# A fused attention and softplus layer: pairing the first blocks of two sequences, with their bias on TensorE and a new order of the work

## The chip, the cores and the metric

The kernel runs on one core of one Trainium2 chip. The metric is device time in microseconds (us) from start to end of one execution, lower is better; three executions of the kernel before gave a median of 213.77 us. The engines are TensorE (PE; its weight loads are shown apart as PEld), VectorE (DVE), ScalarE (ACT), GpSimd (POOL), and SyncE (SP), which here does nothing but issue DMAs. The DMAs that move the data run on 16 DMA engines.

## What is computed

Attention over 4 sequences of 768 tokens with 8 heads of 64, where a token sees the last 96 tokens of its sequence and the first 8 (the global ones), with a linear distance bias per head; then two matrix products with a softplus between them.

```
scores = q @ k^T / sqrt(64)
rel = pos[:, None] - pos[None, :]
is_global = pos[None, :] < 8
is_local = (rel >= 0) & (rel < 96)
dist = where(is_global & ~is_local, 96, abs(rel))
scores = where(is_global | is_local, scores - slope[h] * dist, -1e9)
a = softmax(scores) @ v                 # (4, 8, 768, 64)
x = a.transpose(0, 2, 1, 3).reshape(3072, 512)
h = x @ w_in                            # w_in (512, 2048)
g = max(h, 0) + log1p(exp(-abs(h)))     # softplus
out = g @ w_out                         # w_out (2048, 512)
```

All inputs and the output are float32; the matrix products run in bf16.

## The kernel before

**Tiling.** The 3072 tokens are cut into 24 blocks of 128, six to a sequence. Two blocks are a unit, loaded and transposed together; `UNITS` lists the 12 units in the order in which they are worked. Block n is the n-th in that order, and units and groups have the same numbers: group g of the second half of the layer takes blocks 2g and 2g+1. A block attends to itself and to the block before it in its sequence (256 keys); the first block of a sequence has only itself (128 keys). The 8 global tokens are copied, by `globals_k` (gk) and `globals_v` (gv), into places of the block before that are out of the local window.

**Order.** Nothing is scheduled when the program is built. `ORDER` is one list of words "operation:engine" (P, V, A, G, S for PE, DVE, ACT, POOL, SP), and each engine gets its operations in just this order; an operation that must wait holds up all that stand behind it on its engine. `PLACED` makes the list a table, and dependencies follow from the keys that each operation reads and writes. The names, with unit or block and part as numbers:

- `ldq`, `ldk`, `ldv`: loads of a unit; `win`, `wout`: loads of one of 8 pieces of 512 KB of w_in or w_out (two of them make a column chunk of w_in); `cin`, `cout`: their casts to bf16 (L627).
- `castq`, `castk`, `castv`: casts to bf16. `trq`, `trk`: transposes of q and k, on PE for units 0 to 2 (L740, evicted from PSUM by `cpq`, `cpk`, L747), by DMA later (L763, L770).
- `sb`: the bias put into PSUM by a matmul with the identity (L812, L856); `sc`: scores (L822, L875); `z`: the bias added by DVE where it is not in PSUM (L901); `ex`: the exponential on ACT (L835, L908); `pv`: times v (L927); `nm`: the division (L938, L939); `xt`, `xc`: x transposed into `XT`.
- `a g.p`: one of 8 parts of h = x w_in for group g (L985), `e` and `ln` on ACT: softplus as log(1 + exp(h)) (L1000, L1011); `b`: g w_out (L1032 for groups 0 and 1, L519 later, where seven products of sums take the place of eight, with `ws` and `ka`, L414 and L449, making the sums).
- `fill`: 35 matmuls of zeros (L1145), put where PE was thought to be idle.
- `biasFalse`, `biasTrue`: tiles of bias per head, for first blocks and for others, built on DVE, ACT and POOL.

**Loads.** A unit's q, k or v is 512 KB. For units 0 to 2 (`WIDE`) q and k come in two loads of 256 KB, each partition getting 8 tokens of one head, 2 KB in one run (L582). All else is one load with 512 B runs (L592). In the first stretch the queue holds, in this order, with the two halves of q0 on ACT's queue and the rest on SP's:

```
k0.1 k0.0 q1.0 v0 q1.1 k1.0 win0 k1.1 win1 v1 k2.0 win3 win2 k2.1 q2.0 q2.1
win5 win4 win7 win6 wout0 wout1 v2 wout3 wout2 wout4 wout5 q3 wout6 k3 wout7
```

Later loads are held back by `gates`: each waits for a named product of an earlier group. Loaded data lie in 13 slots (`raw`), used in turn.

**The first stretch on PE**, cut after b0.0.2:

```
fill0 ... fill9 trk0 trq0 fill10 sb0 fill11 ... fill14 sc0 fill15 sb1.0 fill16 sc1.0 sb1.1 pv0.0 sc1.1 fill17 pv0.1
fill18 trq1 fill19 trk1 fill20 pv1.0 pv1.1 fill21 fill22 xt0 sc2 fill23 fill24 fill25 xt1 fill26 fill27 sc3.1 sc3.0
fill28 a0.1 pv2.0 a0.0 fill29 a0.3 fill30 pv2.1 trq2 trk2 xt2 fill31 a0.2 fill32 fill33 pv3.0 a0.5 a0.4 pv3.1 sc4
a0.7 xt3 a0.6 b0.0.0 a1.1 a1.0 b0.0.2
```

a0.0 and a0.1 need both win0 and win1 cast, a0.2 and a0.3 win2 and win3, and so on: a0.7 is the first that needs win6. b0.0.0 needs wout0.

Of the kernel before, what the change touches and what calls it, by code (L numbers as in the profile page):

```python
# [68 lines left out]
ldq0.1:A iota:G ldk0.1:S ldq0.0:A ldk0.0:S dl1a:V blank:V table:A ldq1.0:S dl1c:V fill0:P dl0a:V ldv0:S dl0b:V  # L69
fill1:P dl0c:V ldq1.1:S fill2:P dl1e:V d0:G ident:G fill3:P ldk1.0:S biasTrue2:A d0e:V fill4:P ones:G fill5:P  # L70
biasFalse2:V fill6:P biasFalse7:A biasFalse5:G biasFalse1:V castk0.1:A fill7:P biasFalse6:V biasTrue0:A fill8:P
biasFalse3:A win0:S castk0.0:V biasTrue4:A fill9:P castq0.1:A castq0.0:V ldk1.1:S trk0.0:P biasTrue7:V castq1.0:A
win1:S biasFalse0:V biasFalse4:A trq0.0:P ldv1:S cpk0.0:V fill10:P ldk2.0:S sb0.0:P cpq0.0:A biasTrue3:V fill11:P
castv0.00:G win3:S cpk0.1:V cpq0.1:A fill12:P fill13:P biasTrue1:A fill14:P biasTrue6:G biasTrue5:V sc0.0:P fill15:P
sb1.0:P castv0.11:G ex0.0:A win2:S castv0.01:V fill16:P ex0.1:A sc1.0:P castv0.10:G ldk2.1:S castq1.1:V sb1.1:P
ex1.0:A pv0.0:P sc1.1:P nm0.0:V fill17:P ldq2.0:S ex1.1:A castk1.0:V pv0.1:P fill18:P castk1.1:V ldq2.1:S trq1.0:P
nm0.1:V fill19:P trk1.0:P cpq1.1:V fill20:P cin1:G win5:S pv1.0:P cpk1.0:A cpq1.0:V pv1.1:P fill21:P cpk1.1:A
fill22:P nm1.0:V xt0:P nm1.1:V sc2.0:P fill23:P castv1.11:A castv1.01:G win4:S fill24:P z2.1:V fill25:P xt1:P
gv4.0:A castv1.10:G fill26:P win7:S z2.0:V fill27:P sc3.1:P xc1:A xc0:V cin0:G sc3.0:P ex2.0:A fill28:P z3.0:V
ex2.1:A win6:S castv1.00:G a0.1:P cin3:A castk2.0:G z3.1:V wout0:S pv2.0:P a0.0:P cin2:G e0.1:A wout1:S fill29:P  # L80
nm2.0:V a0.3:P e0.0:A castq2.0:G ldv2:S castk2.1:V ln0.0:A castq2.1:G wout3:S fill30:P pv2.1:P nm2.1:V gk4:G ex3.0:A
trq2.0:P trk2.0:P cin5:G wout2:S cpq2.1:V xt2:P e0.3:A fill31:P a0.2:P cpk2.0:V xc2:A gv4.1:G wout4:S cin4:V
fill32:P fill33:P e0.2:A pv3.0:P cpk2.1:V a0.5:P ex3.1:A cin7:G wout5:S nm3.0:V a0.4:P cpq2.0:V e0.5:A ln0.1:A
pv3.1:P cin6:V sc4.0:P gv8.1:G nm3.1:V a0.7:P ldq3:S e0.4:A z4.0:V ln0.2:A cout0:G wout6:S xt3:P a0.6:P xc3:V e0.7:A
gk8:G z4.1:V b0.0.0:P e0.6:A cout1:G ldk3:S a1.1:P ln0.3:A ws0.1:V a1.0:P ws0.6:V e1.1:A b0.0.2:P castv2.01:G
wout7:S ws0.4:V e1.0:A a1.3:P ex4.1:A castv2.00:G ws0.3:V a1.2:P ldv3:S e1.3:A gk5:G fill34:P ex4.0:A castv2.10:G
sc5.0:P ws1.4:V a1.5:P cout3:G e1.2:A z5.0:V cout2:A pv4.0:P a1.4:P cout4:G e1.5:A nm4.0:V sc5.1:P ln1.0:A ws2.6:V
pv4.1:P b0.0.4:P ws0.7:V a1.7:P e1.4:A gv5.0:V ln1.1:A ws2.7:G z5.1:V b1.0.0:P b1.0.2:P cout5:A b0.0.6:P ws1.7:V
castv2.11:G b1.0.4:P castq3.0:A a1.6:P gv5.1:V cout6:G ldq4:S nm4.1:V b1.0.6:P ex5.0:A trq3:S b0.1.0:P ws2.4:V xt4:P
e1.6:A b0.0.8:P ws1.1:V castk3.0:A b0.0.10:P b0.1.2:P ws3.6:V b0.1.4:P xc4:A trk3.0:S cout7:V b0.1.6:P e1.7:A  # L90
b0.0.12:P ws2.1:V ln1.2:A b0.0.14:P ws1.3:V pv5.0:P b0.1.8:P ex5.1:A nm5.0:V b0.1.10:P ldk4:S b1.0.8:P ws2.3:V
ln1.3:A gk6:G b0.1.12:P ws1.6:V castv3.11:G ldq5:S pv5.1:P b0.1.14:P trk3.1:S oc0.0.0:V castq4.0:A b1.0.10:P ws3.3:G
nm5.1:V b1.0.12:P oc0.1.0:A b1.0.14:P trq4:S xt5:P oc1.0.0:V sc6.0:P castv3.01:G xc5:A gv6.1:A b1.1.0:P castv3.00:G
ldk5:S z6.0:V a2.1:P gv6.0:A castk4.0:G a2.0:P z6.1:V ex6.0:A trk4.0:S pv6.0:P ex6.1:A b1.1.2:P nm6.0:V b1.1.4:P
e2.0:A st1.0.0:S gk7:G pv6.1:P castv3.10:G e2.1:A ldv4:S sc7.0:P nm6.1:V ldv5:S ln2.0:A ws3.4:G a2.2:P trk4.1:S
z7.0:V b1.1.6:P e2.2:A gv7.0:G a2.3:P z7.1:V xt6:S ex7.0:A gv7.1:G b1.1.8:P castq5.0:G e2.3:A pv7.0:P sc8.0:P
ex7.1:A nm7.0:V gv8.0:G a2.5:P z8.0:V ln2.1:A castk5.0:G pv7.1:P b1.1.10:P e2.5:A nm7.1:V a2.4:P castv4.00:G ex8.0:A
z8.1:V xt7:S castv4.01:G a2.7:P e2.4:A castv4.11:V b1.1.12:P ex8.1:A ldq6:S ws3.1:V pv8.0:P a2.6:P st0.1.0:S ln2.2:A
nm8.0:V trq5:S gk9:G b1.1.14:P castv4.10:V e2.6:A pv8.1:P sc9.0:P e2.7:A nm8.1:V gv9.1:G trk5.0:S castv5.00:A a3.0:P
oc1.1.0:V castv5.11:G ln2.3:A ws3.7:G z9.0:V a3.1:P st1.1.0:S xt8:S e3.0:A b2.3:P ka2.7:V ex9.0:A a3.2:P gv9.0:V  # L100
st0.0.0:S ka2.5:G z9.1:V e3.1:A ldv6:S b2.4:P ldk6:S e3.2:A ka2.1:V trk5.1:S ex9.1:A pv9.0:P a3.3:P castv5.10:G
gk10:A a3.4:P ln3.0:A nm9.0:V ka2.6:V pv9.1:P e3.3:A sc10.0:P nm9.1:V gv10.0:G oe2.a:A a3.5:P e3.4:A z10.1:V ka2.2:G
xt9:S b2.1:P e3.5:A ex10.1:A a3.6:P ldq7:S oe2.1:V ldv7:S gv10.1:G a3.7:P ln3.1:A z10.0:V gk11:G castv6.11:G b2.5:P
# [45 lines left out]
WIDE = (0, 1, 2)  # L149
# [1151 lines left out]
```

## Time and profile before

| What | Value |
|---|---|
| Runs | 213.77, 213.84, 212.75 us; median 213.77 |
| The profiled execution | 212.39 us, of which the span from first to last instruction is 210.6 us |
| TensorE clock granted over the span | 0.999 |
| Start to 10 us: PE busy, DMA share | 7.03 us, 0.81 |
| 10 to 20 us | 9.39 us, 1.06 |
| 20 to 30 us | 8.98 us, 1.07 |
| 30 to 40 us | 10.00 us, 1.10 |
| 70 to 80 us | 8.70 us, 1.12 |
| 80 to 200 us | 9.89 us or more in every 10 |
| First part of h = x w_in (a0.1) | starts at 18.69 us |
| a0.7 | starts at 28.94 us |
| Last filler | starts at 35.28 us |
| Load of 256 KB of q or k, issue to landing, median | 7.5 and 6.6 us |
| Load of 512 KB of w_in, issue to landing, median | 9.3 us |

The busy time of PE includes the fillers, and neighbouring matmuls overlap in it, so a full stretch is one in which nothing more fits in, not one without waste. The DMA share is the mean over the 16 DMA engines of the time in which their packets were under way; with several at once it can be over 1. In a timeline, each row is a start, a duration, an engine, a line of the kernel and an operation, "out<-in", and in brackets how long the engine sat idle ahead of it and what ended that.

### The profile page before, as it was taken

The page shows a single profiled execution, that of the slowest core. Times are in us where ns is not written, and L with a number is a line of the kernel's source. Part 1 is how long each engine was busy: PE and PEld are TensorE (multiplying, and loading weights), DVE is VectorE, ACT ScalarE, POOL GpSimd, SP SyncE. Part 2 cuts the span into 40 slices and gives each one's busy share as a digit, 9 for nine tenths or more (in the row PEclk, how much of TensorE's full clock was granted, in tenths as well). Part 3 has the DMA queues.
Part 4 walks back from the last instruction along what each step waited for, and adds up shares of the span by engine and source line. Part 5 has one row for each costly group of instructions (what it writes and reads, how often), then busy time and mean ns, then how long its engine had stood idle before and what let it go on. Part 6 is the DMA issues. An engine that isn't in the chain of part 4 may idle for free.

```text
span 210.6 us, 5494 instructions
## 1 busy us (share of the span) xinstructions
PE 201.3 (96%) x2211; PEld 164.4 (78%) x2211; DVE 156.1 (74%) x287; ACT 174.6 (83%) x248; POOL 105.5 (50%) x113
## 2 busy tenths in 40 slices
PE   5898899999999979999999999999999999999993
PEld 2465687655778868888988988888899889888883
DVE  5779699988788965889888878858883976023494
ACT  5768799998999998978789999896997999775710
POOL 4347668745954763455415783502126849129040
PEclk9999999999999999999999999999999999999999
DMA  5999999999999999999999599955641103400205
GB/s 196 337 355 386 387 357 363 336 209 242 221 304 191 221 214 271 240 166 288 209 170 225 180 181 272 146 124 128 153 99 28 25 5 102 150 0 0 103 0 199
DMA packets 70136, 40.98 MB, mean 195 GB/s; under 512 B 30432, under 2 KB 61664, under 8 KB 70112
## 3 DMA queue, kind: packets, MB, share of 16 engines
q1 hardware_dynamic: 69680, 39.99, 76.2%
q10 hardware_dynamic: 432, 0.66, 0.9%
q8 instruction: 17, 0.28, 0.6%
q14 instruction: 7, 0.06, 0.1%
HBM read 27.26 MB, written 6.29 MB: 159 GB/s over the span
## 4 chain that ended last, share of the span: by engine, by line
PE 68%; DMA 13%; POOL 5%; ACT 5%; DVE 4%; issue 2%; ACTq 0%; SPq 0%; POOLq 0%; DVEq 0%
PE h_ps L985 31%; PE o_ps L519 20%; DMA raw<-in_k_dram 5%; PE s_ps L875 4%; PE x_ps L927 4%; PE s_ps L1032 3%; DMA kT<-kb 3%; DMA raw<-in_q_dram 3%; DMA qT<-qb 2%; PE o_ps L1032 2%; POOL raw L449 2%; ACT pb L908 2%; ACT e L1000 2%; ACT g L1011 1%; POOL g L449 1%
## 5 line engine op out<-in xcount | busy, mean ns | idle before, releaser
L985 PE MATMUL h_ps<-XT,w_in_bf 128*128 128x256 bf16 x768 | 95.5, 273 | 1.5 <-POOL w_in_bf L627 1.3
L985 PEld LDWEIGHTS <-w_in_bf 128*128 128x128 bf16 x768 | 72.4, 98 | 13.1 <-POOL w_in_bf L627 1.9
L1000 ACT ACTIVATE e<-h_ps 128x512 f32<-128x512 f32 x96 | 60.2, 636 | 14.3 <-PE h_ps L985 13.9
L1011 ACT ACTIVATE g<-e 128x1024 bf16<-128x1024 f32 x48 | 50.0, 1057 | 0.4
L901 DVE TENSOR_TENSOR z<-s_ps,biasA 128x1024 f32<-128x1024 f32 x38 | 45.8, 1216 | 3.4 <-PE s_ps L875 2.0
L908 ACT ACTIVATE pb<-z 128x1024 bf16<-128x1024 f32 (+1 forms) x44 | 43.2, 992 | 1.1 <-DVE z L901 1.0
L519 PEld LDWEIGHTS <-g 128*128 128x128 bf16 x320 | 30.8, 98 | 3.6
L449 POOL TENSOR_TENSOR raw<-g 128x1024 bf16<-128x1024 bf16 x11 | 23.5, 2142 | 19.3 <-ACT g L1011 12.8
L677 POOL CAST vb<-raw 64x512 bf16<-64x512 f32 x31 | 20.4, 660 | 11.0 <-DMA raw<-in_v_dram 9.1
L449 POOL TENSOR_TENSOR g<-g 128x1024 bf16<-128x1024 bf16 x9 | 19.5, 2171 | 12.3 <-DVE raw L449 9.7
L793 POOL COPY vb<-vb 4x512 bf16<-4x512 bf16 x16 | 9.8, 612 | 31.7 <-PE x_ps L927 30.6
L519 PEld LDWEIGHTS <-raw 128*128 128x128 bf16 x240 | 23.1, 98 | 2.9
L519 PE MATMUL o_ps<-raw,raw 128*128 128x256 bf16 x192 | 24.1, 273 | 0.0
L519 PE MATMUL o_ps<-raw,g 128*128 128x256 bf16 x160 | 20.1, 273 | 0.0
L927 PEld LDWEIGHTS <-pb 128*128 128x128 bf16 x352 | 16.4, 98 | 4.3 <-ACT pb L908 0.9
L939 DVE TENSOR_TENSOR xs<-x_ps,rcp 128x256 bf16<-128x256 f32 x40 | 17.0, 424 | 1.4
L449 DVE TENSOR_TENSOR raw<-g 128x1024 bf16<-128x1024 bf16 x19 | 15.6, 827 | 2.7 <-ACT g L1011 2.7
L519 PE MATMUL o_ps<-w_out_bf,g 128*128 128x256 bf16 x128 | 16.1, 272 | 0.0
L927 PE MATMUL x_ps<-vb,pb 128*128 128x65 bf16 x304 | 15.8, 193 | 0.0
L938 DVE RECIPROCAL rcp<-x_ps 128x4 f32<-128x4 f32 x40 | 7.1, 179 | 10.3 <-PE x_ps L927 10.1
L1145 PE MATMUL x_ps<-blank 128*128 128x512 bf16 x35 | 12.2, 436 | 2.2 <-DVE blank L1084 2.2
L483 DVE TENSOR_TENSOR osb<-osb,o_ps 128x512 f32<-128x512 f32 x8 | 5.5, 686 | 10.3 <-PE o_ps L519 8.1
(109 smaller groups left out, 227.6 us busy)
## 6 DMA issues: line engine op xcount, KB each, us to landing
raw<-in_v_dram SPq DMA_DIRECT2D x12, 512.0 KB, 6.3
out_dram<-osb SPq DMA_DIRECT2D x22, 256.0 KB, 2.5
raw<-in_q_dram SPq DMA_DIRECT2D x9, 512.0 KB, 5.3
raw<-in_k_dram SPq DMA_DIRECT2D x9, 512.0 KB, 5.1
raw<-in_moe_w_in_dram SPq DMA_DIRECT2D x8, 512.0 KB, 9.3
raw<-in_moe_w_out_dram SPq DMA_DIRECT2D x8, 512.0 KB, 9.4
raw<-in_k_dram SPq DMA_DIRECT2D x6, 256.0 KB, 6.6
raw<-in_q_dram SPq DMA_DIRECT2D x4, 256.0 KB, 7.5
```

The source lines that it names most:

```text
L449: (nc.vector if eng == "DVE" else nc.gpsimd).tensor_tensor(dst, a[0], b[0], ALU.subtract)
L519: nc.tensor.matmul(psum(j), lhs[:, f // 2, f % 2, :], w(f), start=(f == 0 and not (chain and j in "267")), stop=(f == 7), skip_group_check ...
L677: copy_on[eng](dst, src)
L901: nc.vector.tensor_tensor(z, src, bias, ALU.add)
L908: nc.scalar.activation(pb[:, 0:nr, :].rearrange("p (y a) b -> p y (a b)", y=2), src, AF.Exp, scale=1.0 / root_d)
L927: nc.tensor.matmul(xv[:, h, :], pb[:, 4 * (h % 2) + 2 * part + h // 2 if lone else u_all * (2 * (h % 2) + h // 2) + u, :], vb_of(prev if u ...
L939: nc.vector.tensor_tensor(xs[:, 4 * part : 4 * part + 4, :], xv[:, :, 0:D], rcp[:][:, :, None].to_broadcast([P, 4, D]), ALU.mult,)
L985: last = nc.tensor.matmul(hv[:, j, :], w_in_bf[:, m, fb * P : fb * P + P], XT[g % NXG][:, m, :], start=(m == 0), stop=(m == NM - 1),)
L1000: nc.scalar.activation(e[:, p % 2, :, :].rearrange("p j (b t r) -> p (j b) r t", b=2, r=2), hb[:].rearrange("p (a r t) -> p a r t", a=4, r=2),
L1011: nc.scalar.activation(gt[:, 2 * p - 2 : 2 * p + 2, :].rearrange("p a t -> p (a t)"), e[:].rearrange("p a j t -> p (a j t)"), AF.Ln, bias=1.0,
L1032: nc.tensor.matmul(bank(key)[:, 0 : z - a], gt[:, fb, ns * P : ns * P + P], w_out_bf[:, fb, a:z], start=(fb == 0), stop=(fb == NFB - 1),)
L1145: nc.tensor.matmul(x_ps[:], blank[:, 0:P], blank[:])
```

## The change

It pairs the blocks differently. `UNITS` now names the first block itself, and a unit that starts at a block below 2 takes the same block of the next sequence as its second one. Unit 0 is the first block of sequences 0 and 1, unit 1 that of sequences 2 and 3, unit 2 the second block of sequences 0 and 1, unit 7 that of sequences 2 and 3; the others are two neighbours as before. Blocks 0 to 3 are thus the four first blocks (before, blocks 0, 2, 12 and 18 were), and all four get their bias on TensorE, from the first-block tile, with one score operation each; before, block 1 got the wider tile on TensorE, and blocks 2 and 3 were added on DVE.

A q or k half load of units 0 to 2 is as large as before, 256 KB in runs of 2 KB, but is drawn from two sequences: its source pattern runs over 8 pairs of sequence and head, then 16 groups of 8 tokens, where it ran over 32 groups, then 4 heads. Partitions are numbered accordingly, and the eviction of the transposes reads PSUM in another order. The v loads of units 0 to 2, and all three of unit 7, are cut in two, one sequence and 64 partitions each, with keys of their own (`rawx`); `half_users` adds these to what later users of a slot wait for.

```diff
-UNITS = [(0, 0), (1, 0), (0, 1), (0, 2), (1, 1), (1, 2), (2, 0), (2, 1), (2, 2), (3, 0), (3, 1), (3, 2)]
+UNITS = [(0, 0), (2, 0), (0, 1), (0, 2), (1, 2), (0, 4), (1, 4), (2, 1), (2, 2), (3, 2), (2, 4), (3, 4)]
...
-PE_BIAS = (0, 1)
+PE_BIAS = (0, 1, 2, 3)
...
-WHOLE = (0, 2, 4, 6, 7, ...)
+WHOLE = (0, 1, 2, 3, 4, 6, 7, ...)
...
-    units = [[(s, 2 * c), (s, 2 * c + 1)] for s, c in UNITS]
+    units = [[(s, b), (s, b + 1) if b > 1 else (s + 1, b)] for s, b in UNITS]
...
+    def half_users(slot):
+        return [u for x in range(2) for u in users(("rawx", slot, x))]
+
+    def src_keys(which, i, slot, xs=range(2)):
+        if units[i][0][1] < 2 and not (i in WIDE and which != "v"):
+            return [("rawx", slot, x) for x in xs]
+        return raw_keys(slot)
...
         s, b0 = units[i][0]
-        sl = slice(P * b0, P * b0 + W)
+        cross = b0 < 2
+        sl = slice(P * b0, P * b0 + (P if cross else W))
...
                             raw[:, 512 * y : 512 * y + 512],
-                            src[y::2, sl, :].rearrange("h (g r) d -> g h (r d)", r=8),
+                            src[s : s + 2].rearrange("s (h y) t d -> y (s h) t d", y=2)[y, :, sl, :].rearrange(
+                                "x (g r) d -> x g (r d)", r=8
+                            ),
...
+            def ld(dst, rows):
                 return nc.sync.dma_start(
-                    raw[:].rearrange("p (h c) -> p h c", h=H),
-                    src[:, sl, :].rearrange("h (p r) d -> p h (r d)", r=2),
+                    dst.rearrange("p (h c) -> p h c", h=H), rows.rearrange("h (p r) d -> p h (r d)", r=2)
                 )
...
+            if cross:
+                since = half_users(slot) + [u for key in raw_keys(slot) for u in users(key)]
+                for x in range(2):
+                    op(f"ld{which}{i}.{x}", "SP", 0.45, rank + 0.01 * z,
+                       lambda x=x, src=src, raw=raw: ld(raw[64 * x : 64 * x + 64, :], src[s + x, :, sl, :]),
+                       dma=(0.93, 30.0), sync=sync, writes=[("rawx", slot, x)], after=since)
+                continue
...
-        return ("kTa", units[i][0][0] % 2) if first_of(i) else ("kT", later.index(i) % NKT)
+        return ("kTa", units[i][0][0] // 2) if first_of(i) else ("kT", later.index(i) % NKT)
...
-            return NVB + 2 * (units[i][0][0] % 2) + n % 2
+            return NVB + units[i][0][0] + n % 2
...
                     dst[:, :, 64 * r : 64 * r + 64].rearrange("p (x m) (g a) -> p x m g a", x=2, a=4),
-                    tr[:, 512 * r : 512 * r + 512].rearrange("p (a x g m) -> p x m g a", a=4, x=2, g=16),
+                    tr[:, 512 * r : 512 * r + 512].rearrange("p (a x m g) -> p x m g a", a=4, x=2, g=16),
```

`ORDER` is replaced as a whole. The loads of the first stretch are now, with both halves of q0 on ACT's queue as before:

```
v0.0 k0.0 k0.1 k1.0 q1.1 v0.1 q1.0 v1.0 k1.1 v1.1 win0 win1 win3 win2 win4 q2.0
win5 win7 q2.1 k2.0 k2.1 win6 wout2 wout1 v2.0 wout3 wout0 v2.1 wout7 q3 wout5 wout4 k3 wout6
```

and PE's list, cut after b0.0.2:

```
fill0 ... fill3 trq0 fill4 trk0 sb0 fill5 sc0 sb1 sc1 fill6 fill7 fill8 pv0.0 fill9 fill10 trq1 pv1.1 pv0.1 fill11 fill12
trk1 fill13 pv1.0 fill14 fill15 fill16 xt0 fill17 xt1 fill18 ... fill21 a0.0 fill22 sb2 sc2 a0.1 fill23 a0.2 a0.3 pv2.0
fill24 sb3 fill25 sc3 a0.5 pv2.1 a0.4 fill26 xt2 fill27 trq2 fill28 pv3.0 trk2 fill29 fill30 fill31 pv3.1 fill32 a0.7
xt3 a0.6 sc4 a1.1 a1.0 fill33 sc5.0 fill34 a1.3 a1.2 sc5.1 b0.0.0 pv4.0 b0.0.2
```

On POOL cin0 and cin1 now stand together ahead of castv1.11 (before: cin1, then two casts of v1, then cin0); cin6 moves from DVE to POOL, and the eight biasTrue tiles are built behind the exponentials of blocks 0 and 1.

More of the change, by code (lines that the diff above doesn't have):

```diff
@@ L74 @@
[L74 to L88, printed above, removed]
```

164 lines of the change are left out of this document (90 added, 74 removed).

## The prediction

> **What bounds the kernel now.** I read the page first, then the busy time by stretches, the timeline of TensorE and GpSimd over the first 36 us, the waits and the DMA issues.
>
> ```profile
> PE 201.3 (96%) x2211; PEld 164.4 (78%) x2211; DVE 156.1 (74%) x287; ACT 174.6 (83%) x248; POOL 105.5 (50%) x113
> ...
> PEclk9999999999999999999999999999999999999999
> DMA  5999999999999999999999599955641103400205
> GB/s 196 337 355 386 387 357 363 336 209 242 221 304 191 221 214 271 240 166 288 209 170 225 180 181 272 146 124 128 153 99 28 25 5 102 150 0 0 103 0 199
> ```
>
> ```profile
> 18.70:28.90 10.20, 9.18 (x113) 7.54 (x113) 8.09 (x17) 8.56 (x13) 6.46 (x10) 1.00 1.06 382
> 28.90:35.50 6.60, 6.60 (x61) 5.33 (x57) 6.43 (x9) 6.51 (x11) 5.27 (x8) 1.00 1.08 366
> 35.50:77.50 42.00, 41.86 (x453) 30.65 (x452) 36.90 (x62) 40.38 (x56) 27.75 (x33) 1.00 1.15 249
> 77.50:79.10 1.60, 0.30 (x5) 0.07 (x4) 0.13 (x1) 1.57 (x3) 0.52 (x1) 1.00 0.65 145
> 79.10:207.30 128.20, 128.09 (x1440) 112.58 (x1440) 90.35 (x162) 104.86 (x147) 56.92 (x45) 1.00 0.60 138
> ```
>
> ```profile
> 18.69 1.05 PE L985 MATMUL h_ps<-XT,w_in_bf 128*128 128x256 bf16 x8 [0.53 <-POOL w_in_bf L627]
> ...
> 28.94 1.05 PE L985 MATMUL h_ps<-XT,w_in_bf 128*128 128x256 bf16 x8
> ...
> 35.28 0.38 PE L1145 MATMUL x_ps<-blank 128*128 128x512 bf16 x1
> ```
>
> ```profile
> 14.51 1.03 POOL L627 CAST w_in_bf<-raw 128x1024 bf16<-128x1024 f32 x1 [2.72 <-DMA raw<-in_moe_w_in_dram]
> ...
> 23.97 1.04 POOL L627 CAST w_in_bf<-raw 128x1024 bf16<-128x1024 f32 x1 [0.51 <-DMA raw<-in_moe_w_in_dram]
> ...
> 26.76 1.04 POOL L627 CAST w_in_bf<-raw 128x1024 bf16<-128x1024 f32 x1 [1.07 <-DMA raw<-in_moe_w_in_dram]
> ...
> 28.01 0.69 DVE L627 CAST w_in_bf<-raw 128x1024 bf16<-128x1024 f32 x1
> ```
>
> The columns of a stretch are PE, PEld, DVE, ACT and POOL busy, granted clock, DMA share, GB/s. From 28.9 to 207.3 us TensorE is busy all the time but for one wait of 1.3 us at 77.6, at full clock; behind it come only two DVE additions and the last stores (3.3 us). So the end is fixed by two numbers: how late TensorE becomes full, and how much work is then left. Before 35.5 us it does 20 us of real work; the other 15.4 are 35 filler matmuls of 0.216 us each (7.6) and 7.8 of waiting. What it waits for are casts of loaded data, and those wait for the DMA, whose mean share is 0.93 to 1.08 until 35.5 us. **The first 35 us are paced by the arrival of 12 MB, and all that follows by TensorE.**
>
> I turn the GB/s slices (5.265 us each) into a running sum: 1.03 MB at 5.3 us, 2.81 at 10.5, 4.68 at 15.8, 6.71 at 21.1, 8.75 at 26.3. Adding up the loads in queue order gives each its place: v0 ends at 1.84 MB and its first cast starts when the sum is 2.21 (8.79 us); w_in piece 1 ends at 3.67 MB and its cast starts when the sum is 4.22 (14.51 us); piece 5, place 6.82, at 7.84 (23.97); piece 7, place 7.86, at 8.91 (26.76). A load lands once the sum is 0.4 MB, later 0.55 and then 1.0 MB past its place. The last one, piece 6, has place 8.39 and lands by 28.0; its DVE cast (28.01) releases a0.7 at 28.94.
>
> **The change, part by part.**
>
> *Bias on TensorE.* Before: 4 seeds of 256 columns (0.44 us) and 4 of 512 (0.87). After: 16 of 256, 1.75 us. TensorE **+0.44 us**. DVE loses the additions z2 and z3, 1.28 + 2.36 = 3.6 us; at 17.4 to 20.2 us TensorE waits for loads, not for them, so I count nothing, though ex2 and ex3 can start that much sooner.
>
> *Scores, values, transposes, global copies.* Counts are unchanged: four first blocks of 8 score matmuls, twenty others of 16. The eviction reads TensorE's transposed columns in another order, but still 4 values 128 apart at the innermost; nearest rows are DVE 0.68 us, ACT 0.53. Bounds 0 and, at double, 12 x 0.6 us on ACT and DVE inside the load-bound stretch; I take 0.
>
> *v in halves, and unit 7.* Six more SP issues of 0.4 to 0.6 us. Ten issues, not six, precede w_in piece 0 on SP: its issue goes from 4.92 to about 6.9 us. It lay some 7 us in the queue behind other bytes, so this costs nothing while the queue is full, 2 us if it weren't. Behind them on SP only more loads wait. The three extra issues for unit 7 (some 1.5 us of SP near 70 us) come before the transposes for unit 6, whose kind caused the 1.3 us wait at 77.6: 0 to 1.5, taken as 0. Added dependencies only name slots already empty.
>
> *Order of loads.* All twelve q/k halves, v0, v1 and the eight pieces still precede or include piece 6, so its place stays 8.39 MB: equal bytes, 28.0 us. What moves up is little: piece 1 slips to 4.19 MB, landing near 16.1; its POOL cast no longer stands behind castv1, so a0.0 starts near 17.2 instead of a0.1 at 18.69. That lead is gone at a0.7, which again needs piece 6, now cast on POOL (1.04, not 0.69): 29.15 us, **+0.2**.
>
> *Order on TensorE.* What is left once a0.7 starts? Before it, a0.0 to a0.5, six transposes, seeds, scores and xt0 to xt2 are done in both; but before also had sc4.0 (0.55) and all of sc3, pv0 to pv3 with the longer windows: 13.4 us in all, after 12.6, of a total that is 0.44 larger. So 1.3 us more real work follows, and two fillers instead of one (0.22): **+1.5**. wout0 is now the fourth w_out piece, at 10.75 MB: about 35 to 36 us, cast by 37; b0.0.0 comes up near 36.4. At most 0.7 more; I take 0.
>
> *Source pattern of the wide loads.* The twelve q/k half loads of units 0 to 2 keep 256 KB and 2 KB runs, but the outer count of the source goes from 32 (groups of 8 tokens) to 8 (sequence and head), with 16 groups inside. No row of this trace has such a load; all its plain loads and stores have one of 32 or 128, which 16 divides. Lower bound 0: the 256 KB rows as they are (6.6 and 7.5 us to landing). Upper bound: if work is dealt out by the outer count, eight of the 16 engines carry all 3.15 MB, 0.393 MB each instead of 0.197. An engine at 360 to 387 GB/s over 16 moves 0.0225 to 0.0242 MB/us, so the 0.197 MB costs 8.1 to 8.7 us, all ahead of piece 6. A part of it is returned if the laggards, which make the lag grow from 0.4 to 1.0 MB (0.6/0.36 = 1.7 us), are among the idle eight: 6.4. I take this end, since an outer count that 16 divides is the one thing that all the full-rate loads share, at **+7.2**, the middle of 6.4 and 8.1.
> [...]
>
> **Sum.** 7.2 + 0.2 + 1.3 + 0.2 = 8.9 us. Everything behind a0.7 is shifted with it, the later loads too, since those are gated on TensorE's own products. Profiled span 210.6 + 8.9 = 219.5. That execution took 212.39, and the median of the runs is 213.77, 3.17 above the span: **222.7 us**. Own range 219 (a delay of 3.5, if engines that run alone are quicker than any slice here shows) to 225.5 (8.7, and 1.3 more from b0 or unit 7).
>
> **Rivals.**
> *Loads spread as before.* Then only +1.7 remains, and up to 0.7 for wout0: 215.5 to 216.2, with unit 7 worst 217.7. For it: equal bytes and equal runs. Against: the outer count. If the wait at 77.6 also goes, 214.2.
> *Faster.* The 1.0 MB lag is one of uneven engines; v in halves and first blocks first may land piece 6 with the early lag of 0.4 MB, 1.7 us sooner, at 26.3; with its POOL cast a0.7 starts at 27.4, 1.5 sooner. That pays for the 1.5 of work; with the 1.3 saved at 77.6, since other transposes stand there, the span is 209.3, the time 212.5. It decides at a0.7: with that wait gone a start before 28.7 gains, before 27.6 by over 0.5%. For it: in the old order win0 lands near 12 us and its cast waits for castv1 until 17.59. Against: the lag grew while all loads were alike.
> *The change only moves DVE work.* If biases were what held ex2 and ex3, 3.6 us less DVE would show before 20 us; but a0.1 waits on POOL, so no gain: the second case again.
>
> **How the numbers follow.** First case 0.70, second 0.17, third 0.13. About 0.5% (1.07 us) is what a measurement can tell. Slower: 0.70 + 0.8 of the second case = 0.84; the same: the rest of the second and a sixth of the third, 0.05; faster 0.11. The range 214.0 to 225.5 holds most of the first two cases, about 0.8.
>
> **What would show it.** First case: GB/s under 300 in the second and third slices with w_in casts waiting longer on DMA, a0.0 at 20 us or later, a0.7 near 36, or 33 at the quick end, the first score matmul after 10 us (9.44 now), q/k landing times over 9 us early on. Second: a0.0 near 17, a0.7 near 29. Third: a0.7 before 28. From a0.7 on, gaps on TensorE as before; a new wait of over 2 us there (transposes for units 3 to 7, late w_out) would make every sum wrong, as would piece 6 not being what releases a0.7.

## The result, and the profile after

The changed kernel takes **233.91 us** (median of four runs, 232.57 to 235.61) against 213.26 us for the kernel before on the same chip: a ratio of 1.097, with a 95% interval of 1.088 to 1.107. The change makes the kernel slower, as forecast, but by 20.6 us and not by 9; the time lies outside the range of 214.0 to 225.5. Some executions of a kernel come out slower than its others; the ratios and intervals here leave these out, the medians do not.

The profiled execution took 232.57 us with a span of 230.8, against 210.6 before: 20.2 us to be found in the trace. First the page's slices (5.77 us each): TensorE, its granted clock, the DMA share and what the DMA engines moved.

```profile
span 230.8 us, 5493 instructions
...
PE   3095798399999998999999999999999999999993
...
PEclk9999799999999999999999999999999999999998
DMA  4779978999999979899998997996871311300204
GB/s 87 192 190 199 325 242 227 268 277 306 304 174 273 238 207 227 169 222 261 205 182 212 211 249 141 234 247 164 119 113 31 116 26 50 110 25 1 94 19 164
```

In the first four slices 3.9 MB arrive by 23.1 us (5.77 us x 668 GB/s); before, 7.5 MB had. The DMA digits there (4, 7, 7, 9) say that this isn't only engines kept out of work: in the fourth slice they are busy and still move 199 GB/s. From the ninth slice on TensorE is as full as before. The same stretches as in the table of before (PE, PEld, DVE, ACT and POOL busy, granted clock, DMA share, GB/s):

```profile
0.00:10.00 10.00, 1.89 (x4) 0.44 (x4) 2.10 (x8) 2.92 (x6) 3.08 (x12) 1.00 0.55 122
10.00:20.00 10.00, 6.97 (x51) 4.02 (x53) 3.63 (x13) 4.35 (x8) 1.32 (x3) 1.00 0.84 206
20.00:30.00 10.00, 6.63 (x55) 4.36 (x56) 4.26 (x12) 3.72 (x7) 4.33 (x6) 0.83 1.06 282
30.00:40.00 10.00, 9.27 (x95) 6.64 (x95) 4.83 (x14) 8.82 (x15) 2.34 (x3) 1.00 0.78 225
40.00:50.00 10.00, 5.84 (x67) 4.54 (x68) 5.01 (x10) 5.31 (x8) 3.24 (x5) 1.00 1.08 280
```

The timeline of TensorE shows where the time goes: the waits of over 0.4 us in this stretch, behind the one for the first filler, and the starts of a0.0 (29.16) and a0.7 (45.77).

```profile
12.11 1.03 PE L759 MATMUL s_ps<-ident,qb 128*128 128x128 bf16 x8 [6.25 <-DVE qb L664]
...
19.96 0.62 PE L759 MATMUL s_ps<-ident,qb 128*128 128x128 bf16 x8 [0.86 <-DVE qb L664]
...
24.64 1.03 PE L759 MATMUL s_ps<-ident,kb 128*128 128x128 bf16 x8 [3.37 <-POOL kb L664]
...
29.16 1.04 PE L1004 MATMUL h_ps<-XT,w_in_bf 128*128 128x256 bf16 x8
...
43.03 0.62 PE L759 MATMUL s_ps<-ident,kb 128*128 128x128 bf16 x8 [3.09 <-POOL kb L664]
...
45.77 1.05 PE L1004 MATMUL h_ps<-XT,w_in_bf 128*128 128x256 bf16 x8 [1.13 <-POOL w_in_bf L646]
...
53.71 0.59 PE L1051 MATMUL s_ps<-w_out_bf,g 128*128 128x512 bf16 x2 [0.45 <-POOL w_out_bf L646]
```

The three long waits are for casts of q and k, the halves whose source pattern was changed. a0.7 starts at 45.77 instead of 28.94: **16.8 of the 20.2 us are there before a0.7**. The other 3.4 can be read off too. From a0.7 to its end TensorE is busy for 178.5 us instead of 176.9 (1.6), it stands still for 2.97 us instead of 1.55 (1.4), and behind its last matmul pass 3.5 us instead of 3.2 (0.3). The casts that end the three long waits start at 11.63, 23.98 and 42.35 us, each when its load has landed, and the loads are the half loads of q and k. Of all waits of the kernel (total, number, longest) these are the ones for them, first those of the changed kernel, then the largest of the kernel before:

```profile
POOL kb L664 <- DMA raw<-in_k_dram: 13.6, 4, 5.8
...
DVE qb L664 <- DMA raw<-in_q_dram: 11.1, 4, 5.0
```

```profile
POOL qb L645 <- DMA raw<-in_q_dram: 3.1, 1, 3.1
...
DVE kb L645 <- DMA raw<-in_k_dram: 0.7, 2, 0.5
```

### The profile page after: what moved, and what is told of

The parts are those of the page before. It is cut to its first block, busy times and chain, and to the rows that moved or that the text cites. A ratio compares the mean times of both kernels' runs of the same rounds, so it can differ in the third digit from the quotient of the medians.

```text
span 230.8 us, 5493 instructions
## 1 busy us (share of the span) xinstructions
PE 204.9 (89%) x2211; PEld 166.5 (72%) x2219; DVE 159.6 (69%) x283; ACT 173.1 (75%) x244; POOL 111.0 (48%) x117
## 4 chain that ended last, share of the span: by engine, by line
PE 59%; DMA 22%; ACT 7%; DVE 5%; SPq 3%; issue 2%; POOL 1%; DVEq 0%; ACTq 0%; POOLq 0%
PE h_ps L1004 26%; PE o_ps L519 20%; DMA raw<-in_k_dram 6%; DMA raw<-in_moe_w_out_dram 6%; PE x_ps L946 3%; PE s_ps L894 3%; DMA qT<-qb 3%; DMA kT<-kb 3%; DMA raw<-in_q_dram 2%; DMA XT<-xs 2%; ACT e L1019 2%; ACT g L1030 2%; DVE z L920 2%; PE x_ps L519 2%; ACT pb L927 1%
## 5 line engine op out<-in xcount | busy, mean ns | idle before, releaser
L1019 ACT ACTIVATE e<-h_ps 128x512 f32<-128x512 f32 x96 | 59.4, 634 | 19.9 <-PE h_ps L1004 18.9
L920 DVE TENSOR_TENSOR z<-s_ps,biasA 128x1024 f32<-128x1024 f32 x40 | 48.1, 1218 | 4.1 <-PE s_ps L894 4.1
L927 ACT ACTIVATE pb<-z 128x1024 bf16<-128x1024 f32 x40 | 41.7, 1050 | 2.3 <-DVE z L920 2.2
L449 POOL TENSOR_TENSOR g<-g 128x1024 bf16<-128x1024 bf16 x9 | 20.1, 2237 | 23.4 <-DVE raw L449 23.4
L449 POOL TENSOR_TENSOR raw<-g 128x1024 bf16<-128x1024 bf16 x9 | 19.1, 2128 | 23.0 <-ACT g L1030 18.1
L696 POOL CAST vb<-raw 64x512 bf16<-64x512 f32 x31 | 22.1, 714 | 15.5 <-DMA raw<-in_v_dram 11.7
L449 DVE TENSOR_TENSOR raw<-g 128x1024 bf16<-128x1024 bf16 x21 | 17.3, 843 | 1.6 <-ACT g L1030 1.6
L812 POOL COPY vb<-vb 4x512 bf16<-4x512 bf16 x17 | 11.4, 673 | 10.9 <-PE x_ps L946 5.6
L696 ACT CAST vb<-raw 64x512 bf16<-64x512 f32 x8 | 4.9, 617 | 10.8 <-DMA raw<-in_v_dram 9.4
```

The lines of the kernel that those rows point to most:

```text
L449: (nc.vector if eng == "DVE" else nc.gpsimd).tensor_tensor(dst, a[0], b[0], ALU.subtract)
L696: copy_on[eng](dst, src)
L812: copy_on[eng](vb_of(prev)[sl, :, 0:D], vb_of(first)[sl, :, 0:D])
L920: nc.vector.tensor_tensor(z, src, bias, ALU.add)
L927: nc.scalar.activation(pb[:, 0:nr, :].rearrange("p (y a) b -> p y (a b)", y=2), src, AF.Exp, scale=1.0 / root_d)
L1019: nc.scalar.activation(e[:, p % 2, :, :].rearrange("p j (b t r) -> p (j b) r t", b=2, r=2), hb[:].rearrange("p (a r t) -> p a r t", a=4, r=2),
```

## The experiments

The first theory was the prediction's: the new source of the wide loads runs on 8 DMA engines, and the rest costs some 2 us. It leaves 11 us open. The rivals for them were the order of the loads, a wait on SP, the price of the new source on 16 engines, and the halves of v. The expectations name theories by letters; D is that all rows fall in the same halves of 64 KB of memory, F that the halves of v cost the time; G stands for one thing in `b_vhalf` and for another in `b_gap4` and `b_local`. Eighteen kernels were run, each beside the kernel before, which took 211.9 to 212.8 us there. `k16`, `k16_w2`, `k16_b7`, `a_u2`, `b_k4` and `b_vhalf` compute the same as the kernels that they come from; the others read a part of q, k or v from other tokens and serve for their time alone. Their GB/s between 4 and 12 us, the stretch that is most of it wide loads and v, is the quickest way to read them: 342 in the kernel before, 167 in the changed one.

**All 16 engines for the same tokens.** `k16` puts the 16 groups of 8 tokens outermost; the eviction of the transposes restores the order. Same computation.

```diff
-  "x (g r) d -> x g (r d)", r=8
+  "x (g r) d -> g x (r d)", r=8
...
-  tr[...].rearrange("p (a x m g) -> p x m g a", a=4, x=2, g=16)
+  tr[...].rearrange("p (a g x m) -> p x m g a", a=4, x=2, g=16)
```

> The changed kernel with one edit: the source of the twelve q/k half loads runs over 16 groups of tokens outermost and over the 8 pairs of sequence and head inside (partition numbers and the eviction follow). Theory A (the outer count of 8 confines these loads to half the engines, and that is all but about 2 us of the loss): the first four GB/s slices return to 330 to 390, a0.7 starts near 29 to 30 us, and the time is 215 to 217 us. Theory B (a good part of the loss lies in the new order of the queues, above all in wout2, the first w_out load now, whose slot is free only when the last biasTrue tile is built): GB/s is back as well, but SP still stands 5 us before wout2 and the time is 218 to 223. Theory C (what slows the loads is drawing from two sequences): GB/s stays near 190 and the time near 233.

Measured: 226.62 us, 1.063 [1.053, 1.072], in none of the three ranges. From 4 to 12 us 228 GB/s, and on the timeline:

```profile
35.81 1.05 PE L1004 MATMUL h_ps<-XT,w_in_bf 128*128 128x256 bf16 x8
...
45.37 0.59 PE L1051 MATMUL s_ps<-w_out_bf,g 128*128 128x512 bf16 x2 [1.56 <-POOL w_out_bf L646]
```

The number of engines is worth 7.3 us, and some 14 are left with 16 engines at work.

**Four engines in the kernel before.** `b_k4` puts the 4 heads outermost in its wide loads, and the eviction is adapted: same computation.

```diff
-  src[y::2, sl, :].rearrange("h (g r) d -> g h (r d)", r=8),
+  src[y::2, sl, :].rearrange("h (g r) d -> h g (r d)", r=8),
```

> The kernel before, its own order and its own units, with one edit: the source of the twelve q/k half loads runs over 4 heads outermost and 32 groups inside. If the outer count sets how many engines carry a load: 4 engines, GB/s of the first slices near 100, and a time well above that of the changed kernel, 245 to 265 us. If it is not the count: 213 to 215.

Measured: 242.74 us, 1.141 [1.132, 1.150], somewhat under the range for 4 engines. From 4 to 8 us nearly all that moves is wide loads:

```profile
4.00:8.00 4.00, 2.60 (x7) 0.60 (x4) 0.79 (x4) 0.46 (x2) 0.74 (x2) 1.00 0.26 100
```

A DMA share of 0.26 is 4 of 16 engines, at 25 GB/s each. That the outermost count of the pattern sets the number of engines was the author's inference. The runs agree with it: 0.26 here with a count of 4, and 7.3 us less in `k16` with a count of 16 in place of 8.

The packet records show the number as well. Where almost nothing but packets of wide loads is under way, 8.4 of these are in flight on average in the changed kernel (12 to 14 us), 16.9 in `k16` (6 to 9 us) and 4.2 in `b_k4` (5 to 7 us): about one to an engine.

**SP's wait.** In the changed kernel and in `k16`, SP issues w_in piece 6 (at 30.5 us, in `k16` at 23.0) and then stands still: the load of w_out piece 2 goes to the `raw` slot in which the bias tiles are made, so it waits for the last of them, biasTrue7 on ACT. The waits of SP in the changed kernel:

```profile
SPq L642 <- ACT biasA L1140: 5.1, 1, 5.1
```

`k16_w2` moves this load behind the two halves of v2:

```diff
-  a0.4:P wout2:S castq2.1:G ... ldv2.1:S trk2.0:P
+  a0.4:P castq2.1:G ... ldv2.1:S wout2:S trk2.0:P
```

> As the run before, with wout2 issued after wout0 and v2.1 instead of ahead of wout1. Theory A: within 0.5 us of the run before, as the queue is deep. Theory B: SP no longer waits for a biasTrue tile, and it is 2 to 5 us faster.

A miss: 232.56 us, 1.092 [1.082, 1.102], slower than `k16` by 6. Its timelines of DVE and of TensorE say why:

```profile
45.55 0.69 DVE L646 CAST w_out_bf<-raw 128x1024 bf16<-128x1024 f32 x1 [8.00 <-DMA raw<-in_moe_w_out_dram]
```

```profile
46.64 3.59 PE L1004 MATMUL h_ps<-XT,w_in_bf 128*128 128x256 bf16 x16 [6.90 <-DVE XT L982]
```

The cast of w_out piece 2 stands on DVE ahead of xc3, the copy of x that this product needs. A later load holds up DVE, and DVE holds up TensorE. `k16_b7` takes the cause away instead: biasTrue7 goes up behind biasTrue5.

```diff
-  xc1:V biasTrue5:A fill20:P ... nm2.0:V biasTrue7:A cin7:V
+  xc1:V biasTrue5:A biasTrue7:A fill20:P ... nm2.0:V cin7:V
```

> The 16-outermost version, with the last ACT bias tile (biasTrue7) built right behind biasTrue5, ahead of the casts of w_in, so that the slot which wout2 needs is free some 7 us sooner. If the 4.9 us that SP stands before wout2 are on the path: 2 to 5 us faster than the 16-outermost version. If the loads behind it are hidden by those in flight: within 1 us.

225.49 us, 1.060 [1.051, 1.068]: some 1 us less, within the interval. The same edit on `a_old` below (`a_old_b7`) takes the wait off SP's list and gives 218.38 us, 1.031 [1.026, 1.036], again 1.1 us and again within the interval. So some 1 us is likely, and not shown.

> The changed kernel with the old source of the q/k half loads (the run that did so alone took 219.5) and the last ACT bias tile built some 7 us sooner, behind biasTrue5. If the 4.9 us that SP stands before wout2 are on the path there: 1.5 to 4 us faster, 215.5 to 218. If not: within 1 us of 219.5.

**Whose bytes are late.** `a_u2` gives only unit 2, the last of the wide units, the 8 engines back.

```diff
-  "x (g r) d -> g x (r d)", r=8
+  "x (g r) d -> x g (r d)" if i == 2 else "x (g r) d -> g x (r d)", r=8
```

> The changed kernel, with the 16-outermost source for units 0 and 1 and the 8-outermost one for unit 2 alone (4 of the 12 half loads). Theory A with a delay in proportion to the bytes: a third of the way from the first run of this call to the changed kernel, about +6 us over the first. If it is the early loads that cost (nothing else is in the queue, and TensorE grows cold): under +3 us.

228.19 us, 1.069 [1.059, 1.080], 1.6 more than `k16`, where a third of the bytes would have been 2.4 of the 7.3. With intervals of about 1% to either side this does not tell whether the early loads cost more than their share.

**The new source without the new order, and the reverse.** `b_seq2` is the kernel before with its wide loads taken from two sequences, 16 groups outermost, 8 heads inside. `a_old` is the changed kernel with its wide loads read as before, 32 groups from 4 heads.

```diff
(b_seq2)
-  src[y::2, sl, :].rearrange("h (g r) d -> g h (r d)", r=8),
+  srcs[s : s + 2].rearrange("s (h y) t d -> y (s h) t d", y=2)[
+      y, :, P * b0 : P * b0 + P, :].rearrange("x (g r) d -> g x (r d)", r=8),
(a_old)
-  src[s : s + 2].rearrange("s (h y) t d -> y (s h) t d", y=2)[y, :, sl, :].rearrange("x (g r) d -> x g (r d)", r=8),
+  src[s, y::2, P * b0 : P * b0 + W, :].rearrange("h (g r) d -> g h (r d)", r=8),
```

> The kernel before in its own order, with only the places changed that the twelve q/k half loads read: 128 tokens of 8 heads of two sequences, 16 groups outermost, where it was 256 tokens of 4 heads (the wrong tokens for this kernel's pairing: part of q and k is read from elsewhere, all else is computed as before). Theory D (the addresses: the first 128 tokens of a head are the first 32 KB of a stretch that begins at a multiple of 64 KB, as heads lie 192 KB apart, so all these loads fall on one half of the addresses modulo 64 KB and go at half rate): 2 KB packets take 130 ns or more where these loads run, the first slices stay under 250 GB/s, and the time is 217 to 223 us. Theory E (the new order alone loses the rest): 212 to 214 us.

> The changed kernel with its own order and its v halves, but the twelve q/k half loads read just as in the kernel before: 256 tokens of 4 heads of one sequence, 32 groups outermost (so part of q and k is of other tokens than the pairing needs; sizes and counts are the same). If the source of these loads is what costs, and the order itself only the 1.7 to 2.4 us of the prediction: 2 KB packets at 90 to 100 ns, a0.7 at 29 to 31 us, time 214 to 217. If the order or the v halves cost more by themselves: 218 to 222.

`b_seq2`: 219.80 us, 1.033 [1.024, 1.041]; `a_old`: 219.47 us, 1.035 [1.029, 1.042]. Both are slow, so neither is the whole. The stretch from 4 to 12 us of the first:

```profile
4.00:12.00 8.00, 6.54 (x49) 2.96 (x48) 4.53 (x14) 5.36 (x13) 2.19 (x4) 1.00 1.10 258
```

The DMA share is 1.10: all 16 engines are busy, and each packet is slow. The trace's packet records give the mean time of one (ns), for packets that start in each stretch. Those of 2 KB are of wide loads and, late in the second stretch of some kernels, of w_in; those of 512 B are of v. A dash stands for fewer than 60 packets:

```
                      4 to 8 us            8 to 12 us
                      2 KB    512 B        2 KB    512 B
before                 95       28          96        -
after                 174       48         104       33
k16                   151       45         140       56
b_seq2                136       42         134       35
a_old                  98       30         144       41
a_old_v1               88       27          92       31
b_vhalf                93       37          94        -
b_local               135       45         131       34
b_gap4                 88       28          91        -
b_contig               92       28          93        -
```

**Why the source is slow on 16 engines.** Suspect after suspect was taken away. In `k16` the eight pieces of an engine lie 384 KB apart. `k16_sw` makes that 352 KB, so that neighbouring rows fall in different halves of 64 KB, and `k16_swv` does so for the halves of v too; `b_seq2_p4` is `b_seq2` with 380 KB. `b_seq2_sp` leaves 2 KB free between the pieces that follow each other in a row, and `a_old_v` is `a_old` with v taken as every second 512 B of 256 tokens: is it the narrow stretch of memory that is read?

```diff
(k16_sw; k16_swv likewise for v with S * D, b_seq2_p4 with 2 * S * D - 16 * D in all)
+    def spread(src, head, b, step):
+        flat = src.rearrange("b h t d -> (b h t d)")
+        at, step = head * S * D + P * b * D, step - P * D
+        return flat[at : at + 8 * step].rearrange("(x w) -> x w", w=step)[:, 0 : P * D]
...
+  spread(src, 8 * s + y, b0, 2 * S * D).rearrange("x (g c) -> g x c", c=512),
(b_seq2_sp)
-  y, :, P * b0 : P * b0 + P, :].rearrange("x (g r) d -> g x (r d)", r=8),
+  y, :, P * b0 : P * b0 + W, :].rearrange("x (g u r) d -> g x u (r d)", u=2, r=8)[:, :, 0],
(a_old_v)
-  ld(raw[64 * x : 64 * x + 64, :], src[s + x, :, sl, :]),
+  nc.sync.dma_start(
+      raw[64 * x : 64 * x + 64, :].rearrange("p (h c) -> p h c", h=H),
+      src[s + x, :, P * b0 : P * b0 + W, :].rearrange("h (p u r) d -> p h u (r d)", u=2, r=2)[:, :, 0]),
```

> The 16-outermost version of the changed kernel, its q/k half loads alone read each next head 32 KB less than two heads further on, so that the 8 of a load fall on both halves of 64 KB (other tokens than the layer needs; sizes, runs and counts are the same). Theory D: 2 KB packets in the first 16 us go back to 90 to 110 ns, and it is 4 to 8 us faster than the 16-outermost version. Theory E: no change within 1 us.

> As the run before, with the half loads of v (and of unit 7) staggered in the same way. Theory D: 512 B packets back to 30 ns as well, GB/s of the first four slices 190 to 390 as in the kernel before, another 2 to 5 us, to 214 to 219 us in all. Theory E: no change within 1 us.

> The kernel before, with the two-sequence source and 16 groups outermost of the run that read this way, but every second group of 8 tokens out of 256: the 16 engines read 2 KB pieces 4 KB apart at a time, as in the kernel before, not 32 KB on end (other tokens than needed). If it is the narrow stretch that is slow: 2 KB packets back to 90 to 100 ns, time 211 to 214. If it is the eight heads in a row on each engine, or two sequences: still 218 to 221.

> The kernel before with the two-sequence source, 16 groups outermost, each next of the 8 rows 4 KB closer than two heads (380 KB apart; other tokens than needed). If the pitch of 384 KB makes the 8 rows fall on the same part of the memory: packets near 90 to 100 ns, time 211 to 214. If 8 rows are slow at any pitch: 218 to 221.

> As the run before, and the v halves (64 partitions each, as in the change) read every second 512 B of 256 tokens instead of 128 tokens on end (other tokens than needed). If a narrow stretch read by all engines at once is slow: 512 B packets fall from some 45 to 30 ns and it is 1 to 4 us faster than the run before. If 64 partitions are what is slow, or nothing is: within 1 us.

All five miss: 224.61 us (1.058 [1.051, 1.064]), 223.95 (1.055 [1.049, 1.062]), 218.86 (1.033 [1.026, 1.040]), 218.42 (1.030 [1.024, 1.035]) and 219.69 (1.031 [1.025, 1.038]), each within its interval of the kernel it was made from, with 2 KB packets of 129 to 147 ns in the four that have the two-sequence source. The place of the rows in memory, the pitch between them and the narrow stretches do not explain the loss; a part of 1 to 2 us would be hidden in the intervals (`k16_swv` is 2.7 us under `k16` by the medians, and in `a_old_v` the median 512 B packet from 8 to 12 us fell from 39 to 27 ns).

Then the layout of the source itself. `b_contig` reads each wide load as 256 KB on end, an engine's share, as the pattern is written, in one piece of 16 KB.

```diff
-  src[y::2, sl, :].rearrange("h (g r) d -> g h (r d)", r=8),
+  srcs.rearrange("b h t d -> (b h t d)")[(8 * s + 4 * y) * S * D + P * b0 * D :][0 : P * 512].rearrange(
+      "(g x c) -> g x c", g=16, c=512),
```

> The kernel before, its twelve q/k half loads reading 256 KB on end (other tokens than needed; same sizes and 2 KB per partition). If the slow q/k loads of the two-sequence source come from many distant rows per engine (8 heads in turn instead of 4): packets at 88 to 95 ns, time 211 to 213. If it is that neighbouring engines read neighbouring pieces: 130 ns, 217 to 221.

211.66 us, 0.997 [0.993, 1.000]. So distance between an engine's pieces, or that they don't touch, was left. `b_local` takes the same 256 KB on end and deals it out crosswise, and `b_gap4` is the kernel before with every second group of 512 tokens, so that no two pieces of an engine touch.

```diff
(b_local)
+      "(x g c) -> g x c", g=16, c=512),
(b_gap4)
-  src[y::2, sl, :].rearrange("h (g r) d -> g h (r d)", r=8),
+  src[y::2, min(P * b0, 256) : min(P * b0, 256) + 512, :].rearrange("h (g z r) d -> z g h (r d)", z=2, r=8)[0],
```

> The kernel before with each wide q/k load taken from 256 KB on end, as in the run that cost nothing (211.7 us), but dealt out crosswise: an engine's eight pieces of 2 KB lie 32 KB apart, and the pieces next to each other go to different engines (q and k thus come partly from other tokens than the reference takes). Theory G, an engine's pieces have to touch: 217 to 220 us, 2 KB packets of 125 to 150 ns at 4 to 12 us. Theory H, only rows hundreds of KB apart are slow: 211 to 213.5 us, packets of 91 to 98 ns.

> The kernel before, whose wide q/k loads take 32 groups of 8 tokens from each of 4 heads; here every second group of 512 tokens instead of 32 adjacent ones, so that an engine's two groups of one head no longer touch each other, while it still goes over 4 heads (q and k thus come partly from other tokens than the reference takes). Eight heads with one group each cost 7 to 8 us (218.4 to 219.8), all on end nothing (211.7). Theory G, what counts is that an engine's pieces lie next to each other: 217 to 220 us, 2 KB packets of 125 to 150 ns at 4 to 12 us. Theory H, what counts is the number of distant heads that an engine visits (4 against 8): 211 to 214 us, packets of 93 to 100 ns.

`b_local`: 216.85 us, 1.022 [1.014, 1.030]. `b_gap4`: 213.31 us, 1.003 [0.998, 1.007]. The stretch from 4 to 12 us, of `b_local` and then of `b_gap4`:

```profile
4.00:12.00 8.00, 6.82 (x38) 3.53 (x37) 4.99 (x14) 4.47 (x11) 2.44 (x5) 1.00 1.10 258
```

```profile
4.00:12.00 8.00, 7.72 (x58) 3.81 (x55) 5.10 (x14) 6.03 (x14) 3.25 (x6) 1.00 1.06 367
```

Each theory holds in one run and falls in the other: pieces that don't touch are fast in `b_gap4`, and pieces out of one 256 KB are slow in `b_local`, with the very GB/s of `b_seq2`. By time `b_local` loses least among the slow patterns, 4.0 us over the kernel before where `b_seq2` and its two variants are 5.9 to 7.9 over, so distance may add a part. What the slow patterns on 16 engines share (`b_seq2`, `b_seq2_sp`, `b_seq2_p4`, `k16_sw`, `b_local`), whatever the addresses, is the **shape: 16 groups outermost with 8 separate pieces in each, written to 8 neighbouring partitions**. The patterns without the loss have 32 groups of 4 pieces, or one run. The shape sets the order of source and destination together, and no run took them apart: eight separate places to read in turn, against four, would fit every run as well as eight partitions to write. `b_contig`, as it is written, also has 8 neighbouring partitions in each of its 16 groups and is fast (211.66 us); eight partitions as the cause fit it only if a run on end is dealt out otherwise, which no run shows.

**The halves of v.** `b_vhalf` takes the v of units 0 to 2 in two loads of n = 64 partitions each, back to back, in the kernel before (same computation); `a_old_v1` goes the other way and gives `a_old` one load over 128.

```diff
(b_vhalf)
-  raw[:].rearrange("p (h c) -> p h c", h=H),
-  src[:, sl, :].rearrange("h (p r) d -> p h (r d)", r=2),
+  for x in range(cut):
+      raw[n * x : n * x + n, :].rearrange("p (h c) -> p h c", h=H),
+      src[:, sl, :].rearrange("h (p r) d -> p h (r d)", r=2)[n * x : n * x + n],
(a_old_v1)
-  ldv0.1:S
...
-  ldv1.1:S
...
-  ldv2.1:S
...
+                if i in WIDE:
+                    op(f"ld{which}{i}.0", "SP", 0.45, rank + 0.01 * z,
+                       lambda src=src, raw=raw: ld(raw[:], src[s, :, P * b0 : P * b0 + W, :]),
+                       dma=(1.86, 30.0), sync=sync, writes=[("rawx", slot, 0), ("rawx", slot, 1)], after=since)
+                    continue
```

> The kernel before, computing just what it did, with v of units 0 to 2 in two loads of 64 partitions, one right behind the other (partitions 0 to 63 and 64 to 127, 128 tokens each, as in the change). Theory F (a load into 64 partitions is slow, or slows what runs beside it): 512 B packets of these loads at 40 to 50 ns where the whole ones took 27 to 29, and 2 to 5 us more. Theory G (the halves cost only their issue): 211.5 to 213.5.

> The changed kernel with the wide q/k loads read as in the kernel before (219.47 us so far, 1.035 of before), and now the v of units 0 to 2 in one load over 128 partitions each, at the place of its first half, read from 256 tokens of one sequence as in the kernel before; a part of q, k and v thus comes from other tokens than the reference takes. Adding v halves to the kernel before cost about 4 us (1.018). Theory F, the halves cost the changed kernel as much, because a load over 64 partitions has slower 512 B packets: 215.0 to 216.5 us, a0.7 near 27.5 instead of 30.3, packets of 512 B at 4 to 8 us under 28.5 ns. Rival, in the changed order the halves lie where the queue is full anyway and the loss is in the order of the loads: 218.5 to 220, a0.7 at 30 or later.

`b_vhalf`: 216.63 us, 1.018 [1.011, 1.026], with 512 B packets of 37 ns instead of 28 from 4 to 8 us. `a_old_v1`: 216.76 us, 1.021 [1.014, 1.027], 2.7 us less than `a_old`, with packets of 27 and 31 ns and, from 4 to 12 us, 365 GB/s where `a_old` has 292 (its 512 B packets took 30 and 41 ns). The stretch of `a_old`, then of `a_old_v1`:

```profile
4.00:12.00 8.00, 6.33 (x37) 3.45 (x38) 3.98 (x12) 3.75 (x9) 2.20 (x5) 1.00 1.09 292
```

```profile
4.00:12.00 8.00, 6.34 (x37) 3.48 (x38) 4.43 (x13) 3.75 (x9) 2.72 (x5) 1.00 1.09 365
```

The busy share is the same and the bytes differ by a quarter. The time lies between what the two theories asked for (up to 216.5, from 218.5), nearer to the first. The halves cost about 3 us, 4 in `b_vhalf`. They also slow what runs beside them: in `a_old` a 2 KB packet that starts from 2 to 14 us took 97 ns on average with no packet of v in flight and 133 with five or more; in `a_old_v1`, with v whole, it is 89 and 90. Whether it is the 64 partitions or the smaller loads was not taken apart.

**What the order costs alone.** In `a_old_v1` the loads flow as well as before (365 GB/s from 4 to 12 us, 342 in the kernel before), and it is still 2.1% slower. Its timeline from a0.7 on, with all waits of over 0.5 us to the end:

```profile
29.38 1.04 PE L1007 MATMUL h_ps<-XT,w_in_bf 128*128 128x256 bf16 x8
...
37.49 0.59 PE L1054 MATMUL s_ps<-w_out_bf,g 128*128 128x512 bf16 x2 [0.62 <-POOL w_out_bf L649]
...
67.09 1.91 PE L519 MATMUL o_ps<-raw,g 128*128 128x256 bf16 x16 [0.54 <-DVE osb L1083]
71.18 0.40 PE L949 MATMUL x_ps<-vb,pb 128*128 128x65 bf16 x8 [0.66 <-ACT e L1022]
134.99 0.62 PE L897 MATMUL s_ps<-qT,kT 64*128 64x128 bf16 x16 [1.70 <-DMA qT<-qb]
```

The span is 216.1, 5.5 over before (in a run of 217.89 us, its slowest; the others took 216.54 to 216.93). a0.7 is 0.4 late. From there on TensorE is busy for 178.9 us instead of 176.9 (2.0), stands still for 3.95 instead of 1.55 (2.4; the waits shown make 3.5 of it, where the kernel before has one of 1.3), and behind its last matmul pass 3.8 us instead of 3.2 (0.6). But for rounding, that is the whole of the 5.5.

**The sum.** By the ratios, in per cent of some 212.5 us: changed kernel 9.7, `k16` 6.3, `a_old` 3.5, `a_old_v1` 2.1. So of the 20.6 us **about 13 are the new source of the wide loads (7.4 between 8 and 16 engines, 5.8 between the new pattern on 16 engines and the old one), 3.1 the halves of v, and 4.4 order and work**; by the medians the first three are 7.3, 7.1 and 2.7. Each is uncertain by 2 to 3 us, as the intervals are 0.6 to 1% to either side. The two parts of the 13 belong to the way over `k16` and do not lie side by side in the changed kernel: with no packet of v in flight its own 2 KB packets (from 2 to 14 us) took 86 ns in the median and 105 on average (84 and 95 in the kernel before), where those of `k16`, alone from 6 to 9 us, took 138. With packets of v in flight they took 139 to 171 ns on average. No version of the change beats the kernel before.

## Why the prediction was right or wrong

- **What bounds the kernel**: right. The loads pace TensorE until it is full, and all that follows is shifted: 16.8 of 20.2 us stand before a0.7.
- **Eight engines, +7.2**: that an outer count of 8 leaves these loads eight engines was the author's assumption, and no run showed it when the forecast was made. The runs bear it out: 8.4 packets of wide loads in flight where they run alone, 16.9 in `k16`, 4.2 in `b_k4`. The difference to 16 engines is 7.3 us, but that the two numbers agree is luck. The term was to be the price of the new source against the old loads at full speed, and this is about 13.
- **The step that failed** is the size of this term, in the paragraph on the source pattern: both its bounds, 0 and 8.1 to 8.7, lie under the 13. (For the source, v in halves and all the rest the forecast had 7.2, 0 and 1.7; the runs give about 13, 3 and 4.4.) The lower one ("the 256 KB rows as they are") fails by the runs on 16 engines: the rows keep 256 KB and 2 KB runs, and still cost 5.8 to 7.1 us in the new order and 4 to 8 in the old one as soon as they are dealt out in 16 groups of 8. The upper one took each engine at 22.5 to 24.2 GB/s, the rate of the old loads. In the changed kernel the packets of 2 KB took 174 ns instead of 95 between 4 and 8 us. An estimate from the packet records (2 KB packets over 8 engines, those of 512 B over 16) gives each of the eight 13 GB/s from 2 to 6 us, 20 from 6 to 10 and 22 from 10 to 14. So the eight came near the old rate only late, and their packets were slow beside the halves of v. A kernel with eight engines and v whole was not run, so how much of the missing 6 us comes from the halves is open.
- **v in halves "costs nothing"**: wrong by 3 us. The six issues on SP were priced, at 0 to 2; that the halves make packets slower, their own and those beside them, was not. SP issued w_in piece 0 at 13.71 us and not at 6.9 (8.48 in `a_old`, 6.62 in `a_old_v1`): the prediction had SP run ahead of the loads, and its issues were held up with them.
- **Order of loads, "equal bytes"**: nearly right for a0.7, +0.4 in `a_old_v1` where 0.2 was forecast. The first product of w_out was allowed 0.7 more and taken at 0; what SP waits for there, the slot of the bias tiles, was missed; it may be worth 1 us.
- **+1.3 work and +0.2 filler**: right in kind and a little low. TensorE is busy 1.6 us longer behind a0.7 in the changed kernel and 2.0 in `a_old_v1`; no run measured it alone.
- **Bias on TensorE, evictions in another order, unit 7**: no wait points to them. The old wait of 1.3 us for a transposed k is gone, and in the changed kernel no wait behind a0.7 is over 0.66 us; in `a_old_v1` the longest late one is 1.7 us for a transposed q at 135 us.
- **Rivals**: with loads spread as before, 215.5 to 216.2 was forecast (217.7 at worst) and `a_old_v1` measured 216.76, but it needs the v halves undone as well; with the old source alone `a_old` took 219.47. Faster is excluded.
- **What would show it**: GB/s under 300 in the second and third slices (192, 190), a0.0 after 20 us (29.16), the first score matmul after 10 (15.71 for 9.44) were right in direction. a0.7 "near 36" was 45.77, which said at once that another cost of the same kind was missing.

## What to carry to other kernels

When a load is rearranged, price its pattern and not only its bytes and run length: how many engines it gets (7.3 us here between outermost counts of 8 and 16), into how many groups and pieces it is cut (5.8 to 7.1 us here for 16 groups of 8 against 32 of 4), and how many partitions each transfer covers (about 3 us here for the halves of v, 64 partitions and smaller loads together). Where no row of the trace shows the new pattern, zero is no safe lower bound for its cost, and the rate of the old pattern no safe upper one (here 0 and 8.1 to 8.7, and the runs gave about 13); a run with the new pattern alone in the old kernel answers it at once. Check for every load that reuses a buffer who used that buffer last, and on which queue the wait will stand.

## What the runs showed of the hardware

TensorE's granted clock fell where loads starved it, to 0.62 and 0.53 behind a wait of 3.37 us. The changed kernel, TensorE alone (busy, granted clock, DMA share, GB/s), and two rows of its timeline:

```profile
24.00:26.00 2.00, 1.36 (x11) 0.62 1.01 315
26.00:28.00 2.00, 2.00 (x13) 0.53 1.06 388
28.00:30.00 2.00, 2.00 (x18) 1.00 0.97 350
```

```profile
19.96 0.62 PE L759 MATMUL s_ps<-ident,qb 128*128 128x128 bf16 x8 [0.86 <-DVE qb L664]
...
24.64 1.03 PE L759 MATMUL s_ps<-ident,kb 128*128 128x128 bf16 x8 [3.37 <-POOL kb L664]
```

Eight transposes of this kind took 0.62 us behind waits of 0.86 and 3.09 us (at 43.03) and 1.03 behind one of 3.37. Those at 12.11, behind 6.25 us of waiting, took 1.03 as well, though the record gives a clock of 1.00 there: the duration tells more than the record. These need not have slowed down, though, for the four fillers ahead of that wait took 1.89 us, where four took 1.03 at 28.29, at a clock of 1.00, and in `k16` the first transposes took 1.03 behind only 1.54 us of waiting. In `b_k4`, where TensorE is busy for 0.44 us from 8 to 16 us, the clock over the span is 0.943, and 0.50 from 12 to 20 us. So the late load of k at 24.64 seems to have cost twice, by the wait of 3.37 us and by slow matmuls behind it (1.03 us for 0.62). The record has a clock of 1.00 from 42 to 44 us, behind the wait of 3.09; what length of wait brings the clock down was not shown.

DMA share was no measure of speed here: 1.10 with 258 GB/s in `b_seq2` and `b_local`, 1.06 with 367 in `b_gap4`, the same bytes in the same size of packet.
